# The clamp of a weight conversion on GpSimd instead of VectorE, and another PSUM bank for one attention product

## Chip, cores and metric

One core of a Trainium2 chip runs the whole kernel in one launch. The metric is the device time in microseconds (us). Engines are named PE (TensorE), DVE (VectorE), ACT (ScalarE), POOL (GpSimd) and SP (SyncE, which issues the DMAs).

## The reference

Three layers follow one another. The attention has 4 batches, 8 heads, 576 positions and a head size of 64; each position sees itself and the 63 before it. The two feed-forward layers work on 2304 tokens of width 512. All arrays are float32; the kernel gets the weights as 64-bit floats that it converts itself.

```python
scores = np.where(mask, q @ k.T / np.sqrt(64), -1e9)        # window of 64
x = softmax(scores) @ v                                     # (2304, 512)
g = x @ w_gate                                              # 512 -> 1536
x = (g * sigmoid(g) * (x @ w_val)) @ w_out                  # 1536 -> 512
h = x @ w_in                                                # 512 -> 2048
out = (h * np.clip(h + 3.0, 0.0, 6.0) / 6.0) @ w_out2       # 2048 -> 512
```

## The kernel before

**Order of the stages.** `first_block` computes the attention of the first 512 tokens (8 groups of 256 query rows and two heads). Then come 36 steps `n`, for three token blocks `t` of 512 and twelve chunks `c` of the first feed-forward's hidden width. A step multiplies the block with a gate tile and a value tile, applies the activation (`silu`, `times_val`), splits the result into an upper and a lower part (`u_hi`, `u_lo`) and, one step late, multiplies with the output tile (`ffn1_out`). Beside this, a step carries one part each of the attention of later tokens: `scores`, `softmax_a`, `softmax_b`, `transposes`, `evac_t`, `values` and `store_x`. The rest of the tokens and the second feed-forward follow after the 36 steps.

**The conversion of the weights.** `w_ops` is a generator that turns the raw 64-bit weights into float32 and splits each tile of 128x512 into two parts. `pump(k)` runs k of its pieces; between two pieces the caller puts other work. For a tile: ACT takes the upper words' absolute value into a float tile `wf` (L129, in `begin`, issued while the tile before is still being worked on) and scales the lower words (L134); DVE clamps `wf` in place (L148), shifts and masks it (L151), puts sign and top bits in (L186) and adds the lower words (L192); two tiles later ACT copies the upper part (L183) and DVE subtracts for the lower part (L199). The first 36 tiles (`NW1`) are the first feed-forward's, three per chunk; the second's follow. There are four `wf` buffers.

**PSUM.** Eight banks: four for `acc`, one each for `g`, `v`, `c`, `d`. In the steps the scores lie in `c` and the transposes in `d`. The values' product of two steps before lies in `c` in block 0 and in `d` in block 1; `store_x` copies it out (L483), and `evac_t` copies the transposes out (L460).

**What sets the order.** `first_block`, step 0 and everything from step 24 on are written out in order by hand (`manual_schedule`). The order of steps 1 to 23 on each engine is drawn up by a planner from modelled costs when the kernel is built. On each engine instructions are then issued in that order, and semaphores hold one until its inputs are there. On POOL stand, before the change, only the masks' set-up and one memset (L1024).

Of the kernel before, what the change touches and what calls it, by code (L numbers as in the profile page):

```python
# [17 lines left out]
ALU = mybir.AluOpType  # L18
# [46 lines left out]
F64_LOW = float(np.array([897 << 20], np.uint32).view(np.float32)[0])  # L65
F64_HIGH = float(np.array([(1151 << 20) - 1], np.uint32).view(np.float32)[0])
# [3 lines left out]
def attention_two_ffn(ctx: ExitStack, tc, qk, qq, v, w, out):  # L70
    nc = tc.nc
# [23 lines left out]
    NW1 = 3 * NC1  # L95
# [13 lines left out]
    def load_ahead(n):  # L109

        while len(w_loaded) <= n + (4 if len(w_loaded) < NW1 else 3):
            w_loaded.append(len(w_loaded))
            w_load(w_loaded[-1])

    def w_ops():

        held, words = {}, {}

        def begin(n):
            held[n] = cv.tile([128, 512], F32, tag="wf", name="wf", bufs=4)
            if raw_of[n] is not None:
                raw = w_raw.pop(raw_of[n])
                both = raw.bitcast(U32).rearrange("p (n t) -> p n t", t=2)
                words[n] = both[:, :, 0], both[:, :, 1]
                nc.scalar.activation(held[n], words[n][1].bitcast(F32), AF.Abs)  # L129

        def begin_low(n):
            if n in words:
                low = words[n][0]
                nc.scalar.activation(low.bitcast(I32), low, AF.Copy, scale=2.0 ** -29)  # L134

        begin(0)
        yield
        begin_low(0)
        yield
        for n in range(NV + 2):  # L140
            raw_n = raw_of[n] if n < NV else None
            new, sums, old = raw_n is not None, n < NV and raw_n is None, n >= 2
            if n < NV:
                f = held[n]
            if new:
                low, high = words.pop(n)
                u = f.bitcast(U32)
                nc.vector.tensor_scalar(f, f, F64_LOW, F64_HIGH, op0=ALU.max, op1=ALU.min)  # L148
                yield
            if new:  # L150
                nc.vector.tensor_scalar(  # L151
                    u, u, 3, 0x3FFFFFFF, op0=ALU.logical_shift_left, op1=ALU.bitwise_and
                )
                yield
            if sums:
                s0, s1 = f[:, 0:256], f[:, 256:512]
                if raw_of[n - 1] is not None:
                    fa, fb = held[n - 2], held[n - 1]
                    nc.vector.tensor_tensor(out=s0, in0=fb[:, 0:256], in1=fb[:, 256:512], op=ALU.add)
                    yield  # L160
                    nc.vector.tensor_tensor(out=s1, in0=s0, in1=fa[:, 0:256], op=ALU.subtract)
                    yield
                else:
                    fa, fb, fs = keep
                    nc.vector.tensor_tensor(
                        out=s0, in0=fa[:, 0:256], in1=fb[:, 0:256], op=ALU.subtract
                    )
                    yield
                    nc.vector.tensor_tensor(
                        out=s1, in0=fa[:, 256:512], in1=fs[:, 256:512], op=ALU.subtract  # L170
                    )
                    yield
            if n + 1 < NV:
                begin(n + 1)
                yield
            if old:
                if n - 2 < NW1:
                    pool = wp if n - 2 in ring else wq
                    t = pool.tile([128, 2, 512], F32R, tag="w", name="wt")
                else:  # L180
                    t = cv.tile([128, 2, 512], F32R, tag="raw", name="ws", bufs=5)
                o_f = held.pop(n - 2)
                nc.scalar.copy(t[:, 0, :], o_f)  # L183
                yield
            if new:
                nc.vector.scalar_tensor_tensor(  # L186
                    out=u, in0=high, scalar=0xC0000000, in1=u,
                    op0=ALU.bitwise_and, op1=ALU.bitwise_or,
                )
                yield  # L190
                i = f.bitcast(I32)
                nc.vector.tensor_tensor(out=i, in0=i, in1=low.bitcast(I32), op=ALU.add)  # L192
                load_ahead(raw_n)
                yield
            if n + 1 < NV:
                begin_low(n + 1)
                yield
            if old:
                nc.vector.tensor_tensor(  # L199
                    out=t[:, 1, :], in0=o_f, in1=t[:, 0, :].bitcast(F32), op=ALU.subtract  # L200
                )
                if n - 2 < NW1:
                    w_tile[n - 2] = t
                else:
                    nc.sync.dma_start(
                        out=w2_d[n - 2 - NW1],
                        in_=t.rearrange("p a n -> p (a n)").bitcast(F32),
                    )
                yield
            if sums and raw_of[n - 1] is not None:  # L210
                keep = fa, fb, f

    w_iter = w_ops()

    def pump(k):
# [104 lines left out]
    def new_x():  # L320
        return xp.tile([128, KC, TB], F32, tag="xr", name="xr")
# [224 lines left out]
    def gate(tb, c, both=False):  # L546

        g, vv = psum("g"), psum("v") if both else None
        for kc in range(KC):
            up_proj(weight(3 * c), g, kc)  # L550
            if both:
                up_proj(weight(3 * c + 1), vv, kc)
        gv[tb, c] = (g, vv)
# [300 lines left out]
    held, ghl, acc2 = {}, {}, {}  # L854
# [155 lines left out]
    with ExitStack() as fixed:  # L1010
# [10 lines left out]
        for n, (t, c) in enumerate(steps1):  # L1021
            if n == 0:
                start.enter_context(tc.manual_schedule())
                nc.gpsimd.memset(mask[64:128, 1, 0:64], MASKED / SCALE)  # L1024
            if n == 1:
                start.close()
            if (t, c) == (2, 0):
                fixed.enter_context(tc.manual_schedule())

            def at(fn, step, *more):  # L1030
                if step in group_at:
                    fn(group_at[step], *more)

            pumps = CONVERT[t] if t + 1 < NB or c < CONVERT_STOP else 0
            if t + 1 < NB and c == 1:
                xr = new_x()
            last = c == NC1 - 1
            gate(t, c, both=last)
            at(softmax_a, n - 1)
            if n >= LAST_STEP:  # L1040
                at(store_x, n - 3, xr)
            pump(pumps // 2)
            at(softmax_b, n - 1)
            pump(pumps - pumps // 2)
            if last and t + 1 < NB:
                for kc in range(KC):
                    split_x(xr, kc, SIZE[t + 1])
            u = silu(t, c)
            if n < LAST_STEP:
                at(values, n - 2, "d" if t else "c")  # L1050
                at(load_v, n - 1)
                at(store_x, n - 2, xr)
            val(t, c)
            pump(pumps)
            times_val(t, c, u)
            hi = u_hi(u)
            pump(pumps)
            uhl[t, c] = (hi, u_lo(u, hi))
            if n:
                ffn1_out(*steps1[n - 1])  # L1060
            if n < LAST_STEP:
                at(transposes, n - 1, "d")
                at(scores, n, "c")
            elif n in group_at or n - 2 in group_at:
                both = psum("c"), psum("d")
                at(transposes, n - 1, "v")
                at(values, n - 2, both[0][:, GT:])
                at(quarter_scores, n, both)
                at(load_v, n - 1)
            at(evac_t, n - 1)  # L1070
            at(load_qk, n + 1)
            if n >= SAVE_FROM and saves:
                save_w(saves.pop(0))
            if t == NB - 1:
                if c == 6:
                    for k, j in ((0, 0), (1, 0), (0, 1)):
                        open_x(k, j)
                if c == 7:
                    open_x(1, 1)
                if c == 10:  # L1080
                    st.close()
                    side = ExitStack()
                    sp = side.enter_context(
                        tc.tile_pool(name="sp", bufs=3, side="right", reuse_waits="tile")
                    )
                    for _ in wide_sums(0):
                        pass
                advance(x_make, X_STEPS.get(c, 0))
# [57 lines left out]
        for i in range(NS * NU + 1):  # L1146
            s, n = divmod(i, NU)
# [70 lines left out]
```

## Time and profile before

| | us |
|---|---|
| median of 3 runs | 921.35 (918.98 to 922.01) |
| the profiled execution | 920.93 |
| its span, first to last instruction | 919.1 |
| PE busy | 891.6 (97%) |
| DVE busy | 701.7 (76%) |
| ACT busy | 418.1 (45%) |
| POOL busy | 2.7 (0%), 14 instructions |

Busy times are of the profiled execution. An engine's average over the span hides that the stages differ: DVE is fullest in the first 160 us, where attention and conversion run beside the products. A wait is put down to the engine whose result came last; idle time of an engine that is not the bound costs nothing.

### The profile page before, as it was taken

How to read it: one execution, taken by the hardware profiler on the slowest of the kernel's cores; microseconds unless marked ns; L12 is line 12 of the kernel's file. 1: busy time of each engine (PE TensorE's matmuls, PEld its weight loads, DVE VectorE, ACT ScalarE, POOL GpSimd, SP SyncE). 2: the span in 40 equal slices, each digit the busy share in tenths (PEclk: the TensorE clock that was granted, in tenths of full speed). 3: DMA queues.
4: the chain of work that ended last, by engine and by line, in shares of the span. 5: the costliest groups of instructions: out<-in, count | busy, mean ns of one | idle time of the engine just before them, and what ended most of it. 6: DMA issues, size and time to landing. Idle time of an engine off the chain costs nothing.

```text
span 919.1 us, 14495 instructions
## 1 busy us (share of the span) xinstructions
PE 891.6 (97%) x5088; PEld 779.9 (85%) x5088; DVE 701.7 (76%) x1629; ACT 418.1 (45%) x994; POOL 2.7 (0%) x14
## 2 busy tenths in 40 slices
PE   5699999999999999999999999999999999999998
PEld 4487788887777778899999999898989898989896
DVE  7899999988887788698888667667666767565654
ACT  7788987665776766344444432222132222211111
POOL 1000000000000000000000000000000000000000
PEclk9799999999999999999999999999999999999999
DMA  8467997787785978315545479765477565485601
GB/s 325 134 196 237 354 352 258 245 296 273 260 307 171 333 279 296 132 60 194 181 146 168 178 303 359 251 217 192 161 293 294 194 207 203 169 311 198 215 24 69
DMA packets 67608, 207.52 MB, mean 226 GB/s; under 512 B 7248, under 2 KB 14416, under 8 KB 67152
## 3 DMA queue, kind: packets, MB, share of 16 engines
q1 hardware_dynamic: 67392, 206.47, 64.6%
q8 instruction: 40, 0.66, 0.3%
q14 instruction: 32, 0.26, 0.1%
q10 hardware_dynamic: 144, 0.13, 0.0%
HBM read 157.16 MB, written 49.41 MB: 225 GB/s over the span
## 4 chain that ended last, share of the span: by engine, by line
PE 65%; DVE 1%; ACT 1%; issue 0%; ACTq 0%; DVEq 0%
PE acc L891 5%; PE acc L892 5%; PE acc L890 5%; PE v L849 3%; PE v L851 3%; PE v L850 3%; PE g L849 3%; PE g L851 3%; PE g L850 3%; PE acc L593 2%; PE acc L594 2%; PE acc L592 2%; PE d L892 1%; PE c L892 1%; PE d L890 1%; PE c L890 1%
## 5 line engine op out<-in xcount | busy, mean ns | idle before, releaser
L870 ACT CAST gh<-g 128x384 fp32r<-128x384 f32 x96 | 49.3, 514 | 195.8 <-DVE g L861 165.2
L872 DVE TENSOR_TENSOR gl<-g,gh 128x384 fp32r<-128x384 f32 x96 | 53.3, 556 | 45.3 <-ACT gh L870 45.2
L593 PE MATMUL acc<-ul,wt 128*128 128x512 f32 (+1 forms) x216 | 81.6, 378 | 0.5 <-DVE ul L570 0.5
L594 PE MATMUL acc<-uh,wt 128*128 128x512 f32 (+1 forms) x216 | 80.4, 372 | 0.0
L892 PE MATMUL acc<-wt,gl 128*128 128x512 f32 x192 | 75.2, 391 | 0.0
L891 PE MATMUL acc<-wt,gh 128*128 128x512 f32 x192 | 75.1, 391 | 0.0
L890 PE MATMUL acc<-wt,gh 128*128 128x512 f32 x192 | 74.7, 389 | 0.0
L592 PE MATMUL acc<-uh,wt 128*128 128x512 f32 (+1 forms) x216 | 73.3, 373 | 0.2 <-ACT uh L565 0.2
L542 PE MATMUL g<-xh,wt 128*128 128x512 f32 x144 | 59.8, 415 | 3.3 <-ACT xh L331 2.8
L429 ACT ACTIVATE y<-y,s 128x128 f32<-128x128 f32 x144 | 56.2, 393 | 12.2 <-DVE s L423 11.9
L134 ACT ACTIVATE raw<-raw 128x512 int32<-128x512 uint32 x68 | 46.0, 677 | 30.9 <-DMA raw<-w_t 30.7
L542 PE MATMUL v<-xh,wt 128*128 128x512 f32 x144 | 57.3, 398 | 0.5 <-DVE u L585 0.4
L543 PE MATMUL g<-xl,wt 128*128 128x512 f32 x144 | 57.5, 399 | 0.2 <-DVE xl L332 0.2
L849 PE MATMUL v<-xh,wt 128*128 128x384 f32 x168 | 56.7, 338 | 0.4 <-ACT q L936 0.4
L544 PE MATMUL g<-xh,wt 128*128 128x512 f32 x144 | 57.1, 396 | 0.0
L849 PE MATMUL g<-xh,wt 128*128 128x384 f32 x168 | 56.6, 337 | 0.0
L544 PE MATMUL v<-xh,wt 128*128 128x512 f32 x144 | 56.5, 393 | 0.0
L851 PE MATMUL v<-xh,wt 128*128 128x384 f32 x168 | 56.4, 336 | 0.0
L851 PE MATMUL g<-xh,wt 128*128 128x384 f32 x168 | 56.4, 336 | 0.0
L850 PE MATMUL v<-xl,wt 128*128 128x384 f32 x168 | 56.3, 335 | 0.0
L850 PE MATMUL g<-xl,wt 128*128 128x384 f32 x168 | 56.3, 335 | 0.0
L543 PE MATMUL v<-xl,wt 128*128 128x512 f32 x144 | 56.2, 390 | 0.0
(214 smaller groups left out, 2274.1 us busy)
## 6 DMA issues: line engine op xcount, KB each, us to landing
wt<-w2d SPq DMA_DIRECT2D x144, 512.0 KB, 4.9
raw<-w_t SPq DMA_DIRECT2D x68, 512.0 KB, 5.0
w2d<-ws SPq DMA_DIRECT2D x48, 512.0 KB, 4.6
wt<-w1d SPq DMA_DIRECT2D x33, 512.0 KB, 4.4
w1d<-wt SPq DMA_DIRECT2D x26, 512.0 KB, 5.3
v<-v_t SPq DMA_DIRECT2D x36, 256.0 KB, 4.5
qk<-qk_t SPq DMA_DIRECT2D x21, 416.0 KB, 5.1
x_out<-ob SPq DMA_DIRECT2D x17, 256.0 KB, 2.1
```

The source lines that it names most:

```text
L542: nc.tensor.matmul(dst, wt[:, 0, col], hi, start=kc == 0, stop=False)
L543: nc.tensor.matmul(dst, wt[:, 0, col], lo, start=False, stop=False)
L544: nc.tensor.matmul(dst, wt[:, 1, col], hi, start=False, stop=kc == KC - 1)
L592: nc.tensor.matmul(a, wt[:, 0, col], hi, start=c == 0, stop=False)
L593: nc.tensor.matmul(a, wt[:, 0, col], lo, start=False, stop=False)
L594: nc.tensor.matmul(a, wt[:, 1, col], hi, start=False, stop=c == NC1 - 1)
L849: nc.tensor.matmul(dst, wt[:, 0, col], hi[:, k, :], start=k == 0, stop=False)
L850: nc.tensor.matmul(dst, wt[:, 0, col], lo[:, k, :], start=False, stop=False)
L851: nc.tensor.matmul(dst, wt[:, 1, col], hi[:, k, :], start=False, stop=k == 1)
L890: nc.tensor.matmul(a, hi[:, row], wt[:, 0, :], start=begin, stop=False)
L891: nc.tensor.matmul(a, hi[:, row], wt[:, 1, :], start=False, stop=False)
L892: nc.tensor.matmul(a, lo[:, row], wt[:, 0, :], start=False, stop=end)
```

## The change

The clamp becomes a small function of the engine. For the first 36 tiles it is issued on GpSimd in `begin`, right behind ACT's copy and thus one tile earlier in the program than before; the piece of the generator where DVE clamped stays, empty, so that `pump` counts as before. The second feed-forward's tiles are clamped on DVE as before. In block 0 the values' product now takes bank `d` instead of `c`.

```diff
+        def clamp(engine, f):
+            engine.tensor_scalar(f, f, F64_LOW, F64_HIGH, op0=ALU.max, op1=ALU.min)
+
         def begin(n):
...
                 nc.scalar.activation(held[n], words[n][1].bitcast(F32), AF.Abs)
+                if n < NW1:
+                    clamp(nc.gpsimd, held[n])
...
             if new:
                 low, high = words.pop(n)
                 u = f.bitcast(U32)
-                nc.vector.tensor_scalar(f, f, F64_LOW, F64_HIGH, op0=ALU.max, op1=ALU.min)
+                if n >= NW1:
+                    clamp(nc.vector, f)
                 yield
...
             if n < LAST_STEP:
-                at(values, n - 2, "d" if t else "c")
+                at(values, n - 2, "d")
```

## Rows read from the trace of the kernel before

**Rows 1.** Busy time by stretches: window, length, then each engine's busy time (instructions).
```profile
0.00:37.20 37.20, 19.84 (x288) 14.66 (x288) 30.46 (x120) 28.37 (x96) 2.69 (x14) 0.92 0.76 262
...
50.00:160.00 110.00, 108.63 (x628) 88.07 (x627) 105.69 (x277) 94.21 (x236) 0.00 (x0) 1.00 0.82 282
160.00:310.00 150.00, 146.60 (x898) 118.51 (x897) 127.28 (x354) 97.26 (x263) 0.00 (x0) 1.00 0.76 266
```
**Rows 2.** DVE in order of time: start us, length us, line, operands, [idle before].
```profile
5.85 0.43 DVE L148 TENSOR_SCALAR wf<-wf 128x512 f32<-128x512 f32 x1 [3.15 <-ACT wf L129]
6.31 0.43 DVE L151 TENSOR_SCALAR wf<-wf 128x512 uint32<-128x512 uint32 x1
...
9.36 0.69 DVE L443 TENSOR_TENSOR y<-y,s 128x512 f32<-128x512 f32 x1
...
16.31 0.28 DVE L423 CUSTOM_DVE_ANT_0 y<-g,mask 128x128 f32<-128x128 f32 x1
...
18.77 0.42 DVE L148 TENSOR_SCALAR wf<-wf 128x512 f32<-128x512 f32 x1
19.11 0.68 DVE L460 COPY pt<-d 128x512 f32<-128x512 f32 x1
...
28.16 0.42 DVE L148 TENSOR_SCALAR wf<-wf 128x512 f32<-128x512 f32 x1
28.62 0.43 DVE L151 TENSOR_SCALAR wf<-wf 128x512 uint32<-128x512 uint32 x1
...
29.37 0.69 DVE L443 TENSOR_TENSOR y<-y,s 128x512 f32<-128x512 f32 x1
...
31.30 0.69 DVE L460 COPY pt<-d 128x512 f32<-128x512 f32 x1
```
**Rows 3.** ACT in order of time.
```profile
5.16 0.66 ACT L129 ACTIVATE wf<-raw 128x512 f32<-128x512 f32 x1 [3.15 <-DMA raw<-w_t]
...
8.54 0.65 ACT L129 ACTIVATE wf<-raw 128x512 f32<-128x512 f32 x1
...
15.72 0.67 ACT L129 ACTIVATE wf<-raw 128x512 f32<-128x512 f32 x1
...
28.31 0.67 ACT L129 ACTIVATE wf<-raw 128x512 f32<-128x512 f32 x1
...
32.78 0.37 ACT L483 COPY xr<-acc 128x256 f32<-128x256 f32 x1 [1.89 <-PE acc L471]
```
**Rows 4.** PE in order of time.
```profile
32.05 0.69 PE L471 MATMUL acc<-pt,v 128*64 128x64 f32 x16 [0.76 <-DVE pt L460]
...
37.20 0.79 PE L542 MATMUL g<-xh,wt 128*128 128x512 f32 x1 [2.83 <-ACT xh L331]
```
**Rows 5.** PE's waits, 37.2 to 160 us: in total, times, longest.
```profile
PE g L542 <- DVE u L578: 0.4, 1, 0.4
PE c L390 <- ACT xr L483: 0.3, 1, 0.3
```
**Rows 6.** PE's waits, 160 to 310 us.
```profile
PE c L390 <- DMA qk<-qk_t: 1.4, 2, 0.9
...
PE d L452 <- ACT xr L483: 0.5, 1, 0.5
```
**Rows 7.** POOL: the groups of a copy and a select; the memset in order of time.
```profile
masks.py:199 POOL TENSOR_SCALAR_AFFINE_SELECT ident<-ident 128x128 f32<-128x128 f32 x1 | 0.3, 292 | 0.1
L359 POOL COPY mask<-mask 64x64 f32<-64x64 f32 x1 | 0.2, 235 | 0.1
...
14.68 0.15 POOL L1024 MEMSET mask<- 64x64 f32 x1 [11.11 <-DVE s L423]
```
**Rows 8.** DVE's groups, 50 to 160 us: busy us, mean ns | idle before.
```profile
L199 DVE TENSOR_TENSOR wt<-wf,wt 128x512 fp32r<-128x512 f32 x30 | 20.5, 685 | 3.5 <-ACT wt L183 3.3
...
L148 DVE TENSOR_SCALAR wf<-wf 128x512 f32<-128x512 f32 x29 | 11.9, 420 | 0.7 <-ACT wf L129 0.5
...
L332 DVE TENSOR_TENSOR xl<-xr,xh 128x512 fp32r<-128x512 f32 x4 | 2.7, 686 | 0.0
```

## The prediction

> **What bounds the kernel now.** I read first the busy time by stretches [rows 1]. From 50 us on TensorE (PE) is the bound: it is busy 108.63 of 110 us in 50 to 160 and 146.60 of 150 in 160 to 310. What can still be won there is its idle time: 1.37 and 3.40 us. In 0 to 37.2 it idles 17.36 us, because the first attention block comes ahead of all products. So a gain needs an earlier first product or fewer holes behind it; whatever VectorE (DVE) saves beside a busy PE is worth nothing.
>
> Second, the order of work of the engines in the first block. DVE starts on the first clamp (L148) at 5.85, having waited 3.15 us for ScalarE (ACT), and from there runs its written order with hardly a pause [rows 2]. The last step that hangs on that order is the copy L460 at 31.30: PE's product behind it starts at 32.05, ACT waits 1.89 us for that product and starts at 32.78 [rows 3, 4]. From there ACT works down its queue, and PE starts the first feed-forward product at 37.20 after 2.83 us of idle for ACT [rows 4]. So up to 1.89 us of a DVE that is earlier at 31.30 come out at 37.20, and all of a later one.
>
> Third, the load of DVE in 50 to 160: 105.69 of 110 us, so 4.31 us of slack, beside a PE that is nearly full and needs this stretch's weight tiles in step with their conversion [rows 1]. Last, PE's waits behind 37.2: for DVE's L578 0.4, for ACT's copy L483 ahead of the scores 0.3 [rows 5]; in 160 to 310 the transposes wait 0.5 for L483 [rows 6].
>
> **The change, part by part.** *The clamp's length on GpSimd.* The trace has no clamp there. Nearest are the copy of 64 elements per partition, 235 ns, and the select of 128, 292 ns [rows 7]: 57 ns for 64 more, so 235 + 448 x 57/64 = 634 ns for 512. Ends: DVE's own 0.42 us [rows 8] and four selects of 128, 1.17 us. I take 0.63, as the copy and the select are the only rows there that read and write a tile. The Trainium skill (GPSIMD Engine Reference, opening text) speaks against the edit: ordinary elementwise work is the wrong thing for GpSimd, VectorE being roughly twice as fast. By that the clamp is 0.84 us, an estimate from that page; by the reckoning below, DVE held meanwhile, the sum would be 924.1.
>
> *Clamp of tile 0.* DVE's next instruction, the shift L151, now waits for GpSimd, with the whole softmax queued behind it on DVE. ACT's copy ends at 5.82 [rows 3], DVE took it up 0.03 later [rows 2]; so GpSimd runs 5.85 to 6.48 and the shift starts at 6.51 instead of 6.31: +0.20 (ends 0 and +0.74).
>
> *Clamps 1 to 3 leave DVE ahead of 31.30.* Two were followed by their own shift, 0.46 us from start to start (28.16, 28.62), one by a copy, 0.34 (18.77, 19.11) [rows 2]: -1.26. The closest of them, tile 2, has its copy done at 16.39 and was clamped at 18.77 [rows 2, 3]; those 2.4 us, filled by DVE's softmax work, cover GpSimd's 0.63. Without that cover each would cost the 0.20 of tile 0 again. Clamps 4 and 5 come after 31.30, where ACT sets the pace: nothing.
>
> *DVE beside a running clamp.* No row shows DVE and GpSimd at work on large SBUF tiles together. Bounds: DVE isn't touched, or any DVE instruction with only SBUF operands waits for the clamp's end. For the second, clamp 1 would run 9.22 to 9.85, with the product L443 at 9.36 held by 0.49; clamp 4 29.01 to 29.64, with L443 at 29.37 held by 0.27; clamps 2 and 3 fall beside four softmax sums (L423) each that read a PSUM bank, clamp 2 those from 16.31 on, with 0.10 and 0.17 us to spare: nothing [rows 2, 3]. So 0 to +0.76; at 1.17 us clamps 2 and 3 stick out too, 1.03 + 0.44 + 0.37 + 0.81 = +2.65. I take half of 0.76, +0.38, since nothing favours either end.
>
> First block: 0.20 - 1.26 + 0.38 = -0.7. Ends: -1.26 (clamp as on DVE, nothing held) and 0.74 - 1.26 + 2.65 = +2.1.
>
> *50 to 160.* 29 clamps leave DVE, 0.34 to 0.42 each, say 0.38: 11.0 us [rows 8]. PE had only 0.4 us of waiting for DVE there [rows 5]; I take half, -0.2. Against it, DVE work on SBUF operands alone (seven groups of whole tiles, L199 the largest, L332 the last but one) sums to 84.3 us of 113.9 without the clamp, 74% [rows 8]. If it is held, each clamp of length L costs DVE 0.74 L and gives 0.38: at 0.63, +0.09 x 29 = +2.5 us, under the 4.31 of slack: nothing. The cover is gone at L = 0.71 us, where 29 x (0.74 L - 0.38) = 4.31.
>
> *Values' product in the transposes' bank (d for c), steps of block 0.* The scores in c no longer wait for L483 (0.3 goes); the transposes in d now do, which steps 12 to 23 already show at 0.5 [rows 5, 6]. Zero, ends -0.3 and +0.5.
>
> *The planner* draws the order of steps 1 to 23 anew, with DVE lighter and a bank dependence moved. Bounds: all of the 4.77 us of holes in 50 to 310 closed, or as much added. I take -0.2, a twentieth, since DVE and ACT are only some of what those holes wait for.
>
> *Other queues.* On GpSimd the memset L1024 (14.68, waiting for a sum) [rows 7] now stands behind clamps 0 to 5, so till about 35 us; its value is needed by the first feed-forward steps' softmax, after 37.2: nothing. DMA loads and stores keep their places in the program: the steps of the conversion are counted as before, with an empty one where the clamp was.
>
> Sum: -0.7 - 0.2 - 0 - 0.2 = -1.1. The profiled execution took 920.93 us (span 919.1 and 1.83 around it), 0.42 under the median of 921.35; so 919.8.
>
> **Rivals.** *B, the relief gets through:* nothing is held, the first block gives its full -1.06 (-1.26 + 0.20), and the new order closes two thirds of the 4.77 us of holes, -3.2: 916.7. For it: DVE is at 96% and ACT's part of the holes hangs behind DVE. Against: the largest named hole of 160 to 310, 1.4 us, waits for DMAs, and DVE's own of 50 to 160 is 0.4 [rows 5, 6].
>
> *C, the clamp holds DVE and decides, slower:* place, 50 to 160, with DVE at 96%. Point from which it decides: 0.71 us for a clamp. Midway from there to the upper end, 0.94 us: 29 x (0.74 x 0.94 - 0.38) - 4.31 = +4.8 on PE's bill, and the first block 0.51 - 1.26 + 0.80 + 0.21 + 0.14 + 0.58 = +1.0: 926.7; at 1.17, 9.8 + 2.1 = +11.9: 932.8. For it: the point lies only 0.08 above my 0.63. Against: W1's tiles are converted ahead of their use, and a held DVE may still do the PSUM work in between. The Trainium skill (SBUF — State Buffer, "Who interferes with whom") has this as a rule: VectorE's second port pair is GpSimd's only one and is locked for a whole instruction, against VectorE instructions with two SBUF inputs or in a two-port mode, while those with at most one SBUF input outside such a mode go on. No row here shows it yet; by it alone, at 0.63, the sum would be 0.4 later, 920.2.
>
> *D, the order is bad:* where the planner puts ACT's copy right ahead of its use, the clamp's length plus two hand-overs, 0.69 us, comes between; DVE waits for it in a quarter of the 29 tiles less the 0.38 saved, 7 x 0.31 = 2.2, half of which reaches PE, and the first block's gain is lost the same way: 920.93 + 1.1 = 922.0. It is also the case in which the edit doesn't relieve DVE at all.
>
> **How the numbers follow.** About 0.3% (2.8 us) is what can be told from no change here. The forecast 42% (own range 918.2 to 922.5), B 28%, C 22%, D 8%. Faster: B and 4 of the forecast, 0.32. Slower: 20 of C and 3 of D, 0.23. Same: 0.45. The range of 8 in 10 reaches into B (915.5) and to C's midway price (926.5); C's upper end and B with every hole closed stay outside.
>
> **What would show it.** Right: 36 instructions on GpSimd of 0.6 to 0.7 us; DVE's L460 some 0.7 us before 31.30 and the first product near 36.5; PE idle in 50 to 160 still 1 to 1.5 us. L443 starting only at a clamp's end shows that DVE is held; clamps over 0.71 us and PE waiting for L199, L578 or L570 in 50 to 160 show C; DVE waiting for GpSimd at L151 shows D. The forecast is wrong if the first product is no earlier and the holes behind it change by over 3 us.

## The result and the profile after

The changed kernel takes 931.98 us (median of 4 runs, 931.15 to 933.57), against 921.68 for the kernel before beside it (918.98 to 922.53): a ratio of 1.0123 on record, interval 1.0106 to 1.0140 (the two medians alone give 1.0112). It is 10 us slower; forecast were 919.8 and a range to 926.5. The profiled execution took 933.57 us with a span of 931.8, against 920.93 and 919.1.

The busy time by stretches of the changed kernel, with the columns of [rows 1]:

```profile
0.00:37.20 37.20, 22.38 (x288) 16.64 (x288) 27.86 (x111) 26.64 (x92) 13.75 (x20) 0.87 0.73 250
...
50.00:160.00 110.00, 108.15 (x625) 88.89 (x625) 105.68 (x254) 94.50 (x236) 60.34 (x28) 1.00 0.82 288
160.00:310.00 150.00, 143.62 (x860) 116.29 (x857) 120.90 (x332) 94.04 (x250) 0.00 (x0) 0.99 0.72 245
```

PE's idle time from 50 to 160 us is 1.85 us, hardly more than the 1.37 of before. It is 6.38 instead of 3.40 from 160 to 310, where GpSimd (the fifth busy time) does nothing any more. Equal windows mislead when one kernel is late, so here is the same table cut at equal points of the work: first feed-forward product, first output product, first copy of block 0's end, activation of step 24, first product of the later tokens. First before, from the second stretch on (the first, to 37.20, is the first of [rows 1]):

```profile
37.20:50.65 13.45, 13.29 (x48) 10.11 (x49) 11.44 (x22) 9.38 (x18) 0.00 (x0) 0.84 0.47 139
50.65:166.20 115.55, 114.18 (x658) 92.89 (x657) 111.24 (x297) 97.55 (x247) 0.00 (x0) 1.00 0.81 278
166.20:286.79 120.59, 118.16 (x699) 95.44 (x698) 102.66 (x283) 79.26 (x214) 0.00 (x0) 1.00 0.77 267
286.79:399.40 112.61, 111.31 (x725) 89.68 (x724) 89.70 (x215) 63.15 (x155) 0.00 (x0) 1.00 0.67 233
```

And the changed kernel:

```profile
0.00:39.00 39.00, 22.38 (x288) 16.64 (x288) 28.83 (x113) 28.44 (x96) 14.59 (x20) 0.86 0.74 253
39.00:55.10 16.10, 15.44 (x49) 11.55 (x50) 13.06 (x22) 10.85 (x20) 6.84 (x4) 0.71 0.43 133
55.10:172.00 116.90, 113.69 (x660) 93.62 (x659) 112.66 (x279) 98.02 (x247) 57.88 (x27) 1.00 0.80 282
172.00:297.26 125.26, 120.24 (x714) 96.96 (x712) 98.35 (x274) 79.16 (x211) 0.00 (x0) 0.99 0.73 249
297.26:411.80 114.54, 110.83 (x707) 89.33 (x706) 89.37 (x214) 63.08 (x154) 0.00 (x0) 1.00 0.64 227
```

The second column, the length, gives the loss by stage: 1.80 + 2.65 + 1.35 + 4.67 + 1.93 us, and 0.3 in the rest: 12.7 between the two profiled executions (10.3 between the medians). Only the first three, 5.8 us, have clamps on GpSimd in them. The other 6.6 come where it is idle; there PE's idle time grows by 2.6 and 2.4 us, and in the first of the two stretches PE is also busy 2.1 us longer. By itself this does not say that the clamps have no part in the 6.6, since a delay can come out later than it arises.

GpSimd and DVE in the first block of the changed kernel, in order of time. Behind the clamp's old place the line numbers are six higher than before: L157, L449 and L466 are the L151, L443 and L460 of [rows 2]; L192 and L198 were L186 and L192, and L443 was L437 (L132, ACT's copy, was L129). GpSimd:

```profile
6.09 1.92 POOL L124 TENSOR_SCALAR wf<-wf 128x512 f32<-128x512 f32 x1 [2.50 <-ACT wf L132]
11.00 1.92 POOL L124 TENSOR_SCALAR wf<-wf 128x512 f32<-128x512 f32 x1 [2.99 <-ACT wf L132]
...
18.18 1.92 POOL L124 TENSOR_SCALAR wf<-wf 128x512 f32<-128x512 f32 x1 [1.71 <-ACT wf L132]
23.70 1.92 POOL L124 TENSOR_SCALAR wf<-wf 128x512 f32<-128x512 f32 x1 [3.61 <-ACT wf L132]
30.49 2.31 POOL L124 TENSOR_SCALAR wf<-wf 128x512 f32<-128x512 f32 x1 [4.87 <-ACT wf L132]
```

DVE:

```profile
8.04 0.43 DVE L157 TENSOR_SCALAR wf<-wf 128x512 uint32<-128x512 uint32 x1 [5.33 <-POOL wf L124]
...
11.09 1.07 DVE L449 TENSOR_TENSOR y<-y,s 128x512 f32<-128x512 f32 x1
12.08 0.68 DVE L198 CUSTOM_DVE_ANT_0 wf<-raw,wf 128x1024 uint16<-128x1024 uint16 x1
...
18.79 0.16 DVE L443 TENSOR_SCALAR s<-s 128x4 f32<-128x4 f32 x1
...
24.05 0.29 DVE L443 TENSOR_SCALAR s<-s 128x4 f32<-128x4 f32 x1
...
30.94 1.10 DVE L192 SCALAR_TENSOR_TENSOR wf<-raw,wf 128x512 uint32<-128x512 uint32 x1
...
32.68 0.69 DVE L466 COPY pt<-d 128x512 f32<-128x512 f32 x1
```

The clamp takes 1.92 us, three times my 0.63. DVE's first shift therefore starts at 8.04 instead of 6.31 (0.18 us of it is ACT's copy, which got its load later). In this block a DVE instruction on SBUF operands is lengthened when it starts just behind the start of a clamp, and not further in: L449, 0.09 us behind it, takes 1.07 for 0.69; L443 at 24.05, 0.35 behind, 0.29 for 0.16; L192, 0.45 behind the start of a clamp that was itself lengthened, 1.10 for 0.69. L443 at 18.79, 0.61 behind, and L198 at 12.08, 1.08 behind, take their usual 0.16 and 0.68. The copy ahead of the last products is 1.38 us late, and PE follows [rows 4]:

```profile
33.42 1.12 PE L477 MATMUL acc<-pt,v 128*64 128x64 f32 x16 [1.02 <-DVE pt L466]
...
39.00 0.79 PE L548 MATMUL g<-xh,wt 128*128 128x512 f32 x1 [2.38 <-ACT xh L337]
```

The product L477 takes 1.12 us for 0.69, at a granted clock of 0.50 against 1.00 (32 to 34 us). Behind it PE stays longer at the lower of its two clocks. From 40 to 50 us, first before, then after, and two microseconds of the latter:

```profile
40.00:50.00 10.00, 10.00 (x42) 8.19 (x43) 7.99 (x16) 5.93 (x11) 0.00 (x0) 0.92 0.47 144
...
40.00:50.00 10.00, 9.43 (x25) 6.95 (x26) 7.10 (x12) 5.30 (x9) 4.38 (x3) 0.59 0.25 59
...
46.00:48.00 2.00, 2.00 (x6) 1.52 (x6) 1.42 (x3) 1.61 (x3) 0.00 (x0) 0.50 0.00 0
```

### The profile page after: what moved, and what is told of

The parts are those of the page before. It is cut to its first block, busy times and chain, and to the rows that moved or that the text cites. A ratio compares the mean times of both kernels' runs of the same rounds, so it can differ in the third digit from the quotient of the medians.

```text
span 931.8 us, 14519 instructions
## 1 busy us (share of the span) xinstructions
PE 897.6 (96%) x5088; PEld 785.1 (84%) x5088; DVE 698.5 (75%) x1593; ACT 420.0 (45%) x994; POOL 79.3 (9%) x50
## 4 chain that ended last, share of the span: by engine, by line
PE 63%; ACT 1%; DVE 1%; DMA 1%; issue 0%; SPq 0%; ACTq 0%
PE acc L897 5%; PE acc L898 5%; PE acc L896 5%; PE v L855 3%; PE g L855 3%; PE v L857 3%; PE v L856 3%; PE g L857 3%; PE g L856 3%; PE acc L599 2%; PE acc L600 2%; PE acc L598 2%; PE d L898 1%; PE d L897 1%; PE c L897 1%; PE d L896 1%
## 5 line engine op out<-in xcount | busy, mean ns | idle before, releaser
L124 POOL TENSOR_SCALAR wf<-wf 128x512 f32<-128x512 f32 x36 | 76.6, 2138 | 63.1 <-ACT wf L132 62.9
L600 PE MATMUL acc<-uh,wt 128*128 128x512 f32 (+1 forms) x216 | 80.4, 372 | 0.0
L598 PE MATMUL acc<-uh,wt 128*128 128x512 f32 (+1 forms) x216 | 77.5, 373 | 0.1
L548 PE MATMUL g<-xh,wt 128*128 128x512 f32 x144 | 60.9, 423 | 5.9 <-DVE u L584 3.5
L550 PE MATMUL g<-xh,wt 128*128 128x512 f32 x144 | 58.5, 406 | 0.0
L571 ACT CAST uh<-u 128x512 fp32r<-128x512 f32 (+1 forms) x48 | 28.5, 593 | 64.6 <-DVE u L591 35.2
```

The source lines that it names most:

```text
L124: engine.tensor_scalar(f, f, F64_LOW, F64_HIGH, op0=ALU.max, op1=ALU.min)
L548: nc.tensor.matmul(dst, wt[:, 0, col], hi, start=kc == 0, stop=False)
L550: nc.tensor.matmul(dst, wt[:, 1, col], hi, start=False, stop=kc == KC - 1)
L598: nc.tensor.matmul(a, wt[:, 0, col], hi, start=c == 0, stop=False)
L600: nc.tensor.matmul(a, wt[:, 1, col], hi, start=False, stop=c == NC1 - 1)
```

## The experiments

Two theories went in. **H**: the clamps on GpSimd cost by themselves (length, hold on DVE). **P**: the planner's order of steps 1 to 23, drawn anew, costs. In the forecasts of e1 to e4 H is called theory S, and the rival K says that the bank costs. "Moved" is at how many of the 4596 places in the built program's list of PE's products another product (by source line, tile names and addresses) stands than in the kernel before; it tells whether the order is another one, not how bad it is.

| run | clamps on GpSimd | bank | moved | median us | ratio to before (interval) |
|---|---|---|---|---|---|
| the change | 0 to 35 | d | 1056 | 931.98 | 1.0123 (1.0106-1.0140) |
| e1 | none | d | 699 | 922.67 | 1.0020 (1.0002-1.0037) |
| e2 | 0 to 35 | c | 1077 | 939.27 | 1.0189 (1.0155-1.0223) |
| e3 | 0 to 5 | c | 0 | 921.21 | 1.0001 (0.9987-1.0015) |
| e4 | 6 to 35 | c | 1077 | 939.49 | 1.0196 (1.0174-1.0218) |
| e5 | none; 36 left out | c | 1095 | 936.10 | 1.0169 (1.0138-1.0200) |
| e9 | 0 to 35, DVE too | c | 641 | 936.02 | 1.0161 (1.0141-1.0182) |
| e10 | 1 to 5 | c | 0 | 919.66 | 0.9991 (0.9978-1.0003) |
| e12 | 0 to 5, 8 | c | 1020 | 927.98 | 1.0085 (1.0064-1.0106) |
| e13 | 0 to 5, 20 | c | 851 | 925.01 | 1.0055 (1.0035-1.0075) |
| e14 | 0 to 17 | c | 1050 | 930.73 | 1.0116 (1.0101-1.0132) |
| e16 | none; tile 8 left out | c | 1020 | 926.22 | 1.0066 (1.0044-1.0088) |

The kernel before had medians of 920.0 to 921.7 beside these.

**Which part of the change.** e1:

```diff
-                at(values, n - 2, "d" if t else "c")
+                at(values, n - 2, "d")
```

> Only the values' product of block 0 moves to bank d; every clamp stays on VectorE. Theory S (the clamp's length on GpSimd costs, at the start and beside VectorE): as before, within 1.5 us of 921.7, first product at 37.2. Rival P (any change to the steps 1 to 23 makes the planner draw a worse order): 925 or more, with new holes in 50 to 300. Rival K (the bank costs): 926 or more, with TensorE waiting for bank d.

e2 is the other part alone, with the bank as before.

> Only the clamps of the first 36 tiles move to GpSimd; the values' product of block 0 stays in bank c. Theory S: 930 to 934, as with both parts, first product near 39.0. Rival K (the bank): 922 to 927. Rival P (the planner's order, a draw): anywhere from 924 to 934, with the first product at 39.0 and step 24 reached late by another amount than the 10.5 us of the change.

The bank alone costs 0.2%: S's forecast held, K's failed, and so did P's (925 or more), so a redrawn order need not cost much. The clamp without it is dearer still, 939.27, above what any theory had said. So the bank is not the cause, and the two parts do not add.

**Which tiles.** e3 and e4 (in e4 the condition is `6 <= n < NW1`; DVE clamps the other tiles, and the bank stays c):

```diff
-                if n < NW1:
+                if n < 6:
                     clamp(nc.gpsimd, held[n])
```

> GpSimd clamps only tiles 0 to 5, those of the attention's first block; the other 30 are on VectorE, the bank stays c. Theory S: the first product 1.8 us late and the low clock 2.6 us longer, so 921.7 + 4.4 = 926, and nothing more behind step 1. Rival (the late start is hidden later, the cost lies beside the steady steps): 922 to 923. Rival P: 928 or more with new holes behind 55 us.

> GpSimd clamps tiles 6 to 35, VectorE tiles 0 to 5; the bank stays c. Theory S: first product at 37.2 as before; what is left of the loss, 8 us, from the steps behind, by VectorE held 0.4 us per clamp and by waits for clamps of 1.9 us: 928 to 931. Rival (all the loss starts with the late first product): 921 to 923. Rival P: anywhere from 920 to 931, with step 24 late by an amount that VectorE's held time doesn't explain.

e3 went against H. Six clamps in the first block leave every list in the order of before apart from the clamps' own places and one load on SP. They cost nothing in the end, though the first product comes at 38.69 there. With tiles 6 to 35 the whole 19 us are there, above the ranges of all three forecasts; e4 has e2's order on PE, DVE and ACT, and in it six clamps more or less make no difference either. My 4.4 us for a late start was wrong as a part of the total: in e3 the delay was worked off behind it, and PE was idle for only 1.22 us from 160 to 310, against 3.40 before:

```profile
160.00:310.00 150.00, 148.78 (x912) 120.96 (x911) 129.96 (x361) 99.78 (x267) 0.00 (x0) 1.00 0.78 270
```

**Without GpSimd.** e5 drops the line that clamps on GpSimd; DVE does not clamp those tiles either.

> The clamp of the first 36 tiles is left out altogether (values outside the range would be converted wrongly); GpSimd does nothing new, VectorE has 36 instructions less, the bank stays c. Theory P (with VectorE's load lowered the planner draws an order of steps 1 to 23 that runs badly): 928 or more, with holes of TensorE near 170 and 300 as with the clamps on GpSimd. Rival H (GpSimd's 1.9 us per clamp and the held VectorE do it): 917 to 921. Rival M (the planner believes GpSimd faster than it is, so its order is only bad with the real clamp): also 917 to 921.

936.10 us, with 36 DVE instructions less and nothing in their place. Its busy times show where: in 50 to 160 PE is as full as before, in 160 to 310 it idles for 14.8 us, at a lower clock for part of it.

```profile
50.00:160.00 110.00, 109.48 (x630) 89.82 (x628) 103.95 (x257) 95.59 (x233) 0.00 (x0) 1.00 0.81 292
160.00:310.00 150.00, 135.19 (x810) 110.20 (x809) 111.81 (x316) 86.60 (x234) 0.00 (x0) 0.95 0.68 228
```

The largest hole, 4.7 us, stands where the planner's part ends and the written order begins; e2 has the same one. PE is nearly idle for 6 us of 8, and DVE (third busy time), idle for 8 us just ahead, is suddenly full. In e2:

```profile
294.00:298.00 4.00, 4.00 (x35) 3.23 (x34) 0.05 (x1) 1.65 (x5) 0.00 (x0) 1.00 0.00 0
298.00:302.00 4.00, 4.00 (x23) 3.34 (x22) 0.00 (x0) 0.00 (x0) 0.00 (x0) 1.00 0.51 172
302.00:306.00 4.00, 1.76 (x23) 1.08 (x21) 3.49 (x15) 2.78 (x11) 0.00 (x0) 1.00 0.25 68
306.00:310.00 4.00, 0.00 (x0) 0.00 (x0) 3.93 (x9) 1.44 (x4) 0.00 (x0) 0.59 0.89 289
```

DVE's idle time there is one wait, for transposes that stand late in PE's order; PE's hole is one wait for DVE behind it:

```profile
302.23 0.69 DVE L466 COPY pt<-d 128x512 f32<-128x512 f32 x1 [8.18 <-PE d L458]
...
310.09 1.09 PE L458 MATMUL v<-ident,y 128*128 128x128 f32 x4 [4.68 <-DVE u L591]
```

Counted at the activation of step 22, e2 has 64 tiles split and 26 groups through the softmax's first part, the kernel before 63 and 27. An attention group was left to the end. This goes with the hole: e2, e4, e5, e14 and e17 are late by one or two groups there, and these five alone have the hole of 4.7 us. The conversion's lead does not: the changed kernel, e9 and e15 have 64 tiles split, 27 groups and no such hole. So this hole is no part of what the changed kernel loses; behind 280 us its longest is 1.6 us.

**One order, two engines.** e6 and e7 take the planner out (before and e2, each with the written order from step 1 on):

```diff
             if n == 1:
                 start.close()
-            if (t, c) == (2, 0):
                 fixed.enter_context(tc.manual_schedule())
```

> The kernel before with steps 1 to 23 in the order written out by hand, so no planner. A base for the next run: 930 to 990, whatever the theory.

> As the run before it, with the clamps of the first 36 tiles on GpSimd: both have one and the same written order, so the difference is the hardware's alone. Theory P: within 4.5 us above the run before it (the late start) or below it, since VectorE is relieved of 36 clamps. Rival H: 8 us or more above it.

961.66 (ratio to before 1.0453, 1.0425 to 1.0481) and 959.81 us (1.0428, 1.0395 to 1.0460). With 36 clamps on GpSimd the kernel is no slower. At equal points of the work (first output product, activation of step 12), e6:

```profile
0.00:51.48 51.48, 34.24 (x336) 25.72 (x337) 41.99 (x140) 36.70 (x110) 2.69 (x14) 0.83 0.66 222
51.48:194.90 143.42, 120.36 (x650) 96.08 (x649) 123.46 (x306) 101.89 (x252) 0.00 (x0) 0.92 0.59 187
```

and e7:

```profile
0.00:54.05 54.05, 35.91 (x337) 26.75 (x338) 41.36 (x133) 36.92 (x110) 21.66 (x24) 0.84 0.64 214
54.05:192.60 138.55, 118.58 (x649) 95.41 (x648) 115.18 (x277) 102.10 (x251) 51.34 (x27) 0.94 0.60 193
```

2.57 us lost at the start, 4.87 won behind it; behind step 12, where the clamps on GpSimd are done, e7 loses 2.2 of this again. This order leaves PE idle often, so the relief of DVE may count for more than in the kernel before; that it isn't a loss is what separates P from H.

**What sets the clamp's length.** e8 adds operations on GpSimd to the kernel before, ahead of the first block (each behind a `for _ in range(2):`, cut here):

```diff
+        nc.gpsimd.memset(t, 1.0)
...
+            nc.gpsimd.tensor_copy(t, t)
...
+            nc.gpsimd.tensor_scalar(t, t, F64_LOW, None, op0=ALU.max)
...
+            nc.gpsimd.tensor_scalar(t[:, :256], t[:, :256], F64_LOW, F64_HIGH, op0=ALU.max, op1=ALU.min)
...
+            nc.gpsimd.tensor_scalar(t, t, F64_LOW, F64_HIGH, op0=ALU.max, op1=ALU.min)
...
+            nc.gpsimd.tensor_scalar(t, t, 1.0, 1.0, op0=ALU.mult, op1=ALU.add)
...
+            nc.gpsimd.tensor_tensor(out=t[:, :256], in0=t[:, :256], in1=t[:, 256:], op=ALU.mult)
```

> The kernel before with thirteen more instructions on GpSimd at the start, on a tile that nothing reads: a memset, and two each of a copy, a maximum alone, maximum and minimum on 256 and on 512 columns, multiply and add on 512, and a product of two halves. What sets the clamp's 1.92 us: if its length goes with the columns alone, the copy also takes about 1.9; if with the operations, the maximum alone takes about half; if maximum and minimum are slow as such, multiply and add is shorter. No theory moves the total by more than 3 us.

The groups of GpSimd, columns as in [rows 7], in the order maximum with minimum, maximum, the same on 256 columns, product, multiply with add, copy:

```profile
L516 POOL TENSOR_SCALAR probe<-probe 128x512 f32<-128x512 f32 x2 | 4.1, 2044 | 0.2
L512 POOL TENSOR_SCALAR probe<-probe 128x512 f32<-128x512 f32 x2 | 3.0, 1512 | 0.2
L514 POOL TENSOR_SCALAR probe<-probe 128x256 f32<-128x256 f32 x2 | 2.1, 1063 | 0.2
L520 POOL TENSOR_TENSOR probe<-probe 128x256 f32<-128x256 f32 x2 | 2.1, 1052 | 0.2
L518 POOL TENSOR_SCALAR probe<-probe 128x512 f32<-128x512 f32 x2 | 1.2, 617 | 0.2
L510 POOL COPY probe<-probe 128x512 f32<-128x512 f32 x2 | 1.2, 612 | 0.1
```

Neither columns nor number of operations alone decide: a copy takes 0.61 us, a multiply with an add 0.62, a maximum alone 1.51 (2.04 is the mean of a clamp of 1.92 and one of 2.17). The total, 923.84 (ratio 1.0040, 1.0022 to 1.0058), moved no more than expected; but the order is that of before, and the first product comes at 39.89, so it seems that a start late enough does reach the end.

**Clamp on both engines.** e9 leaves DVE's clamp in place for all tiles, behind GpSimd's.

> The first 36 tiles are clamped on GpSimd and once more on VectorE, where the clamp stood before; the second changes nothing in the values. The bank stays c. All 36 GpSimd clamps with their length and their hold on VectorE are there, but VectorE is not relieved, so the planner has nearly the load of before. Theory P (the loss is the order drawn for a lighter VectorE): 920 to 927. Rival H (the loss is GpSimd's part): 936 or more, as VectorE now also has its 36 clamps back.

936.02: P's forecast, 920 to 927, failed, and H's held. But the order was not that of before either (641 places moved), so P in the form "a lighter DVE draws the bad order" fell; GpSimd's presence alone redraws it. This kernel loses elsewhere, too: PE waits 2.5 us in 50 to 170 for ACT's weight copies, the changed kernel not at all (e12 and e16 1.6 and 1.8). The run doesn't tell the theories apart.

**Repairs.** e10 puts tiles 1 to 5 on GpSimd (`1 <= n < 6`), e11 is the changed kernel with `CONVERT = (8, 4, 6)` for `(8, 5, 5)`.

> GpSimd clamps tiles 1 to 5 only; tile 0, on which the start waits, and tiles 6 to 35 are on VectorE, the bank stays c. The first block gets its relief without the wait of 1.9 us at the start. Theory P (the order of steps 1 to 23 is drawn as with six tiles, and the start is free): first product near 36.8, 917 to 920. Rival (VectorE's hold eats the relief in the first block): first product at 37.2 or later, 920 to 922.

> The changed kernel with the conversion slower in block 1 and faster in block 2 (pieces per pumping 8, 4, 6 instead of 8, 5, 5). Theory P, in the form that the conversion runs ahead while one attention group falls behind: with fewer pieces in block 1 the attention keeps up, the holes at the change from block 1 to block 2 shrink, 922 to 929. Rival (the order is bad for another reason than the conversion's lead): 930 or more.

e10, 919.66, can't be told from the kernel before; its first product came at 37.52, so the rival was right about the first block. e11 took 937.38 (1.0178, 1.0156 to 1.0200). Slower conversion in block 1 did not close the loss: PE is idle for 5.8 us from 160 to 310, against 6.4, and new waits came in block 2, where transposes wait 7.1 us for `times_val`. That the conversion's lead is the cause is thus not shown, and e9 and e15 above speak against it.

**One instruction.** e12 and e13 add one tile to e3 (`n in (*range(6), 8)`, then 20); e14 has `n < 18`; e16 has nothing on GpSimd and leaves out DVE's clamp of tile 8.

> GpSimd clamps tiles 0 to 5 and tile 8, one single clamp more than the kernel with tiles 0 to 5, which has the order of before on every engine; bank c. This one clamp lies in the planner's part, and behind it the order of TensorE, VectorE and ScalarE is another one. Theory P (the planner's draw decides): the time is that of another draw, 923 to 937, and then with holes of TensorE where no clamp runs. Rival H (cost per clamp on GpSimd): within 1.5 us of 921.

> As the run before it, with tile 20 in place of tile 8: the order differs only from there on. Theory P: another draw for half of the steps, 919 to 935. Rival H: within 1.5 us of 921.

> GpSimd clamps tiles 0 to 17, half of the 36; bank c. Rival H (per clamp, 6 tiles cost nothing, 36 cost 18 us with bank c): about 928 to 930. Theory P: no such line through the number of clamps, anywhere from 920 to 938.

> Nothing on GpSimd: the kernel before without VectorE's clamp of tile 8 alone (that clamp is left out), so 0.4 us less work for VectorE in all. The planner draws the steps anew for it. Theory P (the draw decides, whichever edit causes it): 923 to 932, near the 928 of the run with tile 8 on GpSimd, whose order is a near relative. Rival H (cost of clamps on GpSimd): 919 to 921.

These decide. A seventh clamp at tile 8 costs 8 us (927.98), where six cost none; at tile 20, from where on alone the order differs, 5 us (925.01). Leaving out one DVE instruction of 0.4 us costs about 6 us (926.22), with nothing on GpSimd. No clamp lasts 8 us, and one left out holds nobody. What is more, e12 and e16 have one and the same order on PE, DVE and ACT, apart from the clamps: seven clamps on GpSimd in one, none in the other, and 1.0085 and 1.0066 with intervals that overlap. In this order the clamps' own part can't be told from nothing; the order costs. From 160 to 310, where GpSimd is idle in both, PE idles 4.4 (e12) and 5.9 us (e16), against 3.4 before:

```profile
160.00:310.00 150.00, 145.58 (x894) 117.81 (x894) 127.66 (x343) 99.19 (x260) 0.00 (x0) 1.00 0.76 260
160.00:310.00 150.00, 144.06 (x888) 117.13 (x889) 126.01 (x338) 97.01 (x257) 0.00 (x0) 1.00 0.75 257
```

e14, 930.73, lies in P's range and just above H's line, so by its time alone it tells nothing; its hole of 4.7 us comes more than 200 us after its last clamp on GpSimd.

**The clamp's length.** e15 is the changed kernel, e17 e2, with a short operation in the clamp's place (the clamp is left out):

```diff
-                    clamp(nc.gpsimd, held[n])
+                    nc.gpsimd.tensor_scalar(held[n], held[n], 1.0, 0.0, op0=ALU.mult, op1=ALU.add)
```

> The changed kernel, bank d, with a multiplication by 1 and an addition of 0 on GpSimd instead of the clamp (the clamp is left out): the same place and operands, but 0.62 us instead of 1.92 each. The order is another one again, as the planner knows the shorter operation. Rival H (the clamp's length costs): 919 to 922. Theory P (VectorE's relief changes the order, the length isn't needed): 925 to 937, as without any clamp.

> The 36 clamps replaced by the short operation on GpSimd (0.62 us; the clamp left out), with the values' product of block 0 left in bank c. Against 939 with the real clamp and bank c, and 936 with no clamp at all and bank c. Theory P: 925 to 938, another draw. Rival H (the clamp's 1.92 us is what costs): 919 to 923.

e17, 934.77 (1.0167, 1.0135 to 1.0198): a third of the length, and nearly all of the loss of e2. e15, 924.53 (1.0049, 1.0032 to 1.0066), is 6 to 7 us below the changed kernel against the kernel before beside each (0.74% by the ratios), above H's range and just under P's. Both orders are new again, so the length's share cannot be read off.

## Why the prediction was wrong, step by step

- **The planner's order, -0.2 with ends of 4.77 either way.** The step that failed. I took a redrawn order for a small unbiased shift. In the runs every redrawn order costs: 0.2% (e1) to 2% (e4) in all thirteen kernels that the planner drew anew (eleven orders, since e2 and e4 share one, and e12 and e16), the changed kernel among them, and e1, e5 and e16 with no clamp on GpSimd. Where two kernels have one order and only the clamps differ (before with e3 and with e10, e2 with e4, e12 with e16, e6 with e7), no pair is clearly apart. That the changed kernel's 6.6 us where GpSimd is idle are of this kind is likely, not shown: no run has its order without its clamps. My upper end, as much idle time added as there was, had no ground: e5 adds 11.4 us of it in 160 to 310.
- **The clamp's length, 0.63, ends 0.42 and 1.17.** 1.92, outside both. The copy's price carries over to a copy (0.61) and to multiply with add (0.62), not to maximum and minimum. So of the rivals C's condition was met (over 0.71), and its time, 926.7 to 932.8, covers the result; but not by C's mechanism. C has the loss in 50 to 160, by its own formula 29 x (0.74 x 1.92 - 0.38) - 4.31 = 25.9 us for such a clamp; there PE's idle time grew by 0.5. D's sign was there too, DVE waiting 1.6 us for GpSimd before the shift in 50 to 160, at less than the 2.2 that D reckoned. B, an order that closes holes, was wrong in its direction.
- **Clamp of tile 0, +0.20.** +1.73. The rest of the first block was right in kind and adds up: 1.73, the relief of -1.26, and 0.38 + 0.13 + 0.41 of held DVE make 1.39, and the copy L466 came 1.38 late; one product at the lower clock makes that 1.80 at the first product, where -0.7 was forecast. The lower clock behind it made it 4.45 by the first output product. e3 shows that such a start need not reach the end; e8, which starts 2.7 us late in the order of before, did lose 0.4%.
- **DVE beside a running clamp, +0.38, half of a full hold.** 0.92 in the first block. (The reckoning left out the small L437 and L438, which also have only SBUF operands; with them its upper bound would have been about 1.0 instead of 0.76.) Held were instructions that started early in a clamp, by 0.41 us at most and not for the clamp's length: of the 30 on SBUF operands that start in the first 0.55 us of one of the 36 clamps 23 are lengthened, of the 62 that start later 4, none of them between 0.55 and 1.4 us in. From 50 to 160 the rows of the shift and of L443 show it, first the shift before, then after:

```profile
L151 DVE TENSOR_SCALAR wf<-wf 128x512 uint32<-128x512 uint32 x30 | 12.3, 419 | 0.0
...
L192 DVE SCALAR_TENSOR_TENSOR wf<-raw,wf 128x512 uint32<-128x512 uint32 x31 | 22.4, 722 | 0.1
L198 DVE CUSTOM_DVE_ANT_0 wf<-raw,wf 128x1024 uint16<-128x1024 uint16 x31 | 22.3, 721 | 0.2
...
L157 DVE TENSOR_SCALAR wf<-wf 128x512 uint32<-128x512 uint32 x30 | 15.6, 521 | 1.6 <-POOL wf L124 1.6
...
L443 DVE TENSOR_SCALAR s<-s 128x4 f32<-128x4 f32 x9 | 2.7, 298 | 0.0
```

  By means against the same view of before, the shift lost 30 x 0.102 = 3.1 us, L443 9 x 0.134 = 1.2, L192 and L198 31 x 0.038 = 1.2 each and L576 11 x 0.062 = 0.7: 7.3 in all, two thirds of the 11.0 that the 29 clamps gave. So DVE was still relieved, as the sum had it. The Trainium skill's rule (SBUF — State Buffer, "Who interferes with whom") says that the later of the two fully blocks for the whole instruction; L198 at 12.08, with two SBUF inputs and its usual 0.68 us inside a clamp, goes against it, and the measurement decides. (The profile's times on GpSimd are rough, but DVE starts its first shift at 8.04, 0.03 us after the clamp's recorded end.)
- **The bank, zero.** +0.2%, 1.8 us, alone in e1 (interval 0.02 to 0.37%), with a redrawn order, so above the end of +0.5 us that I gave. With the clamps on GpSimd bank d comes out better (931.98 against 939.27), again with another order.

**Left open.** How much of the 10.3 us the clamp's real length adds in the order that the change has: no run shows it; e15, with the short operation, is 6 to 7 us lower, but has another order. Also why the changed kernel's order runs badly: the late attention group explains a hole in five other kernels, not its own. The order of before with all 36 clamps on GpSimd was not tried.

## What to carry over

Where a planner orders part of a kernel, an edit there changes two things, itself and the order, and the second can be the larger; here each of the eleven new orders was a loss. Price it from runs in which one instruction is added or left out. To learn what the edit itself costs, compare two kernels with one and the same order: a fixed one, a subset of the edit that leaves the order alone, or two edits that draw the same order. An operation's time on another engine is taken from the same operation there, not from one with the same operands.

## What the runs showed of the hardware

- On GpSimd, 128x512 in float32, in SBUF: copy 0.61 us, multiply with add 0.62, maximum 1.51, maximum with minimum 1.92 (the shortest; of the changed kernel's 36, 15 take 1.91 to 1.93 and the longest 3.25); on 256 columns 1.06. DVE's clamp takes 0.42.
- A clamp on GpSimd held DVE instructions on SBUF operands when they started in its first 0.55 us (23 of 30 in the changed kernel, by at most 0.41 us), none of the 28 that started 0.55 to 1.4 us in, and 4 of the 34 later ones. None of the 42 that read a PSUM bank inside a clamp was lengthened. The clamp at 30.49, which began while a DVE instruction on SBUF operands was running, took 2.31 us.
- In the changed kernel PE's granted clock was 0.50 of full speed (1.2 of 2.4 GHz) in every slice of 2 us from 30 to 48 us. PE was busy for 0.6 to 1.0 us of each slice from 32 to 40, and for nearly all of each from 42 on. In the kernel before the clock was 0.50 only from 36 to 40, and back at 1.00 from 42 on.
